# Moving the output stores to ScalarE's queue, letting attention run two batches ahead, and making loads wait for output transposes, in a fused attention and two-layer kernel

## The chip, the cores and the metric

The kernel runs on one core of a Trainium2 chip. The metric is the device time of one execution in microseconds (us); lower is better. A quoted time is a median over executions. A ratio is the mean time of one kernel's fast runs over the mean of the other's fast runs of the same rounds on the same chip, so it is not quite the ratio of the medians quoted beside it. A run is fast unless it lies over 1.5% above the fastest of its kernel.

## The reference

```python
def _attn_ref(q, k, v):              # B, H, S, D = 8, 8, 576, 64
    scores = 1/sqrt(D) * q @ k^T
    # heads 0-3: causal window of 32; heads 4-7: causal window of 128, every 4th key
    attn = softmax(where(mask, scores, -1e9))
    return attn @ v

def _moe_ref(x, w_in, w_out):        # x 4608x512, w_in 512x2048, w_out 2048x512
    h = x @ w_in
    g = h * sigmoid(h)
    return g @ w_out
# x is the attention output with the heads of a token put side by side
```

## The kernel before

All matmuls of attention and of the two layers are issued from one loop. A small model of the engines (`plan`), which runs while the program is built, picks the next step for TensorE; each step's other instructions, the DMAs too, are recorded when the model reaches them. An engine's queue therefore holds its instructions in the order in which the model recorded them.

The words used below:

- **Cast**: GpSimd DMAs that read k and q of a batch as f32 and write them as f16 to a buffer in DRAM (`kq_s`).
- **Turn** of a batch: four DMA transposes on SyncE that bring its k and q from `kq_s` into `nat` and `kqT`.
- **Loads** after a turn: GpSimd waits on a small copy (`fence`) until the turn has landed, then starts v of that batch (`vraw`, `vp`) and the cast of the next.
- **Output transpose**: attention's results (`oP`, `oD`) of batches 2 to 7 are stored to `x_s` in DRAM and read back transposed into `xA` or `xR`, the input of layer 1. A group of layer 1 or 2 has 512 tokens; a batch has 576. Groups 0 and 1 need no output transpose.

```python
    XR = 3                                   # buffers xR
    # ...
    def issue_turn(b):
        # ... (cut)
            nc.sync.dma_start_transpose(out=dst[:, None, :], in_=win)          # nat, x2
        # ... (cut)
            nc.sync.dma_start_transpose(out=kqTs[b % 2][:, i], in_=rows)       # kqT, x2

    def turn_gen(b):
        yield "DMA", max(0.0, TURN_AT.get(b, 0.0) - plan.now)
        issue_turn(b)
        count(("L", b - 2), 2, lambda: loads_after(b))
        yield "DMA", 9.0

    def loads_after(b):
        for i in range(2):
            nc.gpsimd.tensor_copy(fence[:, i : i + 1], kqTs[b % 2][:, i, 1, HN * M - 1 :])
        issue_v(b)
        if b + 1 < B:
            issue_cast(b + 1)

    def group_gen(g):                        # the output transpose of group g
        t0 = max(g * GT, PEB * S)
        n = (g + 1) * GT - t0
        nc.sync.dma_start_transpose(out=x_of(g)[:, :, GT - n :], in_=x_s[t0 : t0 + n])
        yield "DMA", 8.0

    def stored(b):                           # called after each of four stores to x_s
        def then():
            for g in range(NG):
                if need[g] == b:
                    plan.push(groups[g], group_gen(g), plan.now)

        count(("O", b), 4, then)
    # ...
            # after the last score step of batch b: the turn of batch b + 2
            if kind == "S" and b + 2 < B:
                st.after = lambda: count(
                    ("S", b), NS, lambda: plan.push(turned[b + 2], turn_gen(b + 2), plan.t)
                )
    # ... end of a y tile in layer 2
            ob = o32.tile([P, DM], F32, tag="ob", bufs=2, name=f"ob_{g}_{tb}")
            nc.scalar.activation(ob, y, AF.Copy, scale=0.5)
            nc.sync.dma_start(out=out[t0 + tb * P : t0 + (tb + 1) * P], in_=ob)
    # ... which attention steps may be picked while layer 1 is at group g1
        cands = [(att, it, 1.0) for it in att[:LOOK] if it[0] <= g1 + 1]
```

The softmax here doesn't subtract the row's maximum and nothing guards it: scores larger than these inputs give would overflow.

## Time and profile before

| | before |
|---|---|
| time, median (4 runs) | 355.88 us |
| span of the profiled run | 352.8 us |
| mean granted TensorE clock | 0.966 |
| TensorE (PE) busy | 305.7 us, 87% |
| stretches at half clock | 24 us (83.95 to 90.78, 114.67 to 128.33, 152.2 to 155.6) |

The lines that carry the reading stand in the prediction. The question is where TensorE stands still. The prediction's **ledger** and **lag**, which it explains, serve for that: the place of a step in the ledger is the full-clock work ahead of it, in us; a jump of the lag is a stall or half-clock work, and the lag of the last step sets the time.

### The profile page before, as it was taken

The page shows a single profiled execution, that of the slowest core. Times are in us where ns is not written, and L with a number is a line of the kernel's source. Part 1 is how long each engine was busy: PE and PEld are TensorE (multiplying, and loading weights), DVE is VectorE, ACT ScalarE, POOL GpSimd, SP SyncE. Part 2 cuts the span into 40 slices and gives each one's busy share as a digit, 9 for nine tenths or more (in the row PEclk, how much of TensorE's full clock was granted, in tenths as well). Part 3 has the DMA queues.
Part 4 walks back from the last instruction along what each step waited for, and adds up shares of the span by engine and source line. Part 5 has one row for each costly group of instructions (what it writes and reads, how often), then busy time and mean ns, then how long its engine had stood idle before and what let it go on. Part 6 is the DMA issues. An engine that isn't in the chain of part 4 may idle for free.

```text
span 352.8 us, 5672 instructions
## 1 busy us (share of the span) xinstructions
PE 305.7 (87%) x2200; PEld 148.0 (42%) x2200; DVE 201.7 (57%) x477; ACT 153.5 (44%) x258; POOL 48.2 (14%) x76
## 2 busy tenths in 40 slices
PE   0678998992987199789998999999999999999995
PEld 0553544440443044334544444444444444444442
DVE  5594779771775055648866756966675255155100
ACT  1455763442443044445455445545445344244211
POOL 8725000503204002300050030000000000000000
PEclk9999999997899579989999999999999999999999
DMA  8999999999999999995999999051227100100121
GB/s 111 188 205 201 196 190 201 128 192 187 194 199 142 165 233 197 151 163 86 210 156 224 235 172 144 19 123 41 87 64 149 61 0 30 61 30 30 61 82 67
DMA packets 115898, 47.41 MB, mean 134 GB/s; under 512 B 82592, under 2 KB 111264, under 8 KB 115872
## 3 DMA queue, kind: packets, MB, share of 16 engines
q0 software_dynamic: 47152, 19.92, 47.8%
q1 hardware_dynamic: 68720, 27.14, 35.7%
q8 instruction: 17, 0.28, 0.3%
q14 instruction: 9, 0.07, 0.1%
HBM read 39.84 MB, written 20.05 MB: 170 GB/s over the span
## 4 chain that ended last, share of the span: by engine, by line
PE 73%; DMA 14%; DVE 6%; ACT 4%; SPq 1%; issue 1%; POOL 1%; ACTq 0%; POOLq 0%
PE h L611 33%; PE y L639 32%; DMA xR<-x_s 5%; DMA xA<-x_s 3%; DMA x_s<-oD 3%; PE s L413 2%; DMA nat<-in_q_dram 2%; PE av_d L449 2%; DVE oD L453 1%; PE av_p L449 1%; DVE gT L622 1%; SPq L135 1%; ACT th L620 1%; DVE oP L453 1%; ACT ob L650 1%; ACT probs L421 1%
## 5 line engine op out<-in xcount | busy, mean ns | idle before, releaser
L622 DVE SCALAR_TENSOR_TENSOR gT<-th,h 128x512 f16<-128x512 f32 x144 | 97.9, 684 | 92.7 <-ACT th L620 92.7
L639 PE MATMUL y<-w_out,gT 128*128 128x512 f16 x576 | 141.0, 383 | 8.5 <-ACT ob L650 8.1
L620 ACT ACTIVATE th<-h 128x512 f32<-128x512 f32 x144 | 86.2, 599 | 102.0 <-PE h L611 98.7
L611 PE MATMUL h<-xR,w_in 128*128 128x512 f16 x384 | 93.7, 383 | 4.4 <-DMA xR<-x_s 4.3
L611 PEld LDWEIGHTS <-w_in 128*128 128x128 f16 x576 | 54.8, 100 | 81.3 <-issue 22.0
L639 PEld LDWEIGHTS <-gT 128*128 128x128 f16 x576 | 53.6, 98 | 68.5 <-issue 10.2
L611 PE MATMUL h<-xA,w_in 128*128 128x512 f16 x192 | 51.2, 404 | 13.3 <-DMA xA<-x_s 10.2
L421 ACT ACTIVATE probs<-s 128x768 f16<-128x768 f32 (+2 forms) x45 | 36.4, 810 | 22.3 <-PE s L413 22.3
L650 ACT ACTIVATE ob<-y 128x512 f32<-128x512 f32 x36 | 21.5, 597 | 55.1 <-PE y L639 45.3
L449 PEld LDWEIGHTS <-probs 128*128 128x128 f16 x448 | 23.4, 103 | 15.7 <-issue 2.5
L453 DVE TENSOR_TENSOR oD<-av_d,rcps 72x256 f16<-72x256 f32 x64 | 26.9, 421 | 2.2
L300 POOL COPY fence<-kqT 128x1 f16<-128x1 f16 x12 | 2.4, 202 | 142.8 <-DMA kqT<-kq_s 142.8
L453 DVE TENSOR_TENSOR oP<-av_p,rcps 96x256 f16<-96x256 f32 x48 | 20.2, 421 | 1.6
L449 PE MATMUL av_d<-vd,probs 128*128 128x65 f16 x256 | 15.7, 201 | 1.0 <-DVE rcps L452 0.6
L452 DVE RECIPROCAL rcps<-av_p 96x4 f32<-96x4 f32 x48 | 8.4, 174 | 13.2 <-PE av_p L449 13.0
L428 DVE TENSOR_TENSOR probs<-probs,mask_d 128x864 f16<-128x864 f16 (+1 forms) x24 | 13.2, 551 | 3.1 <-ACT probs L421 2.5
L428 DVE TENSOR_TENSOR probs<-probs,mask_p 128x768 f16<-128x768 f16 x24 | 13.3, 554 | 2.6 <-ACT probs L421 2.1
L449 PE MATMUL av_p<-vp,probs 128*128 128x65 f16 x192 | 13.3, 202 | 1.5 <-DVE probs L428 0.9
L452 DVE RECIPROCAL rcps<-av_d 72x4 f32<-72x4 f32 x64 | 11.0, 172 | 5.0 <-PE av_d L449 4.9
L383 PE MATMUL td<-ident,nat 96*128 96x96 f16 x48 | 4.3, 242 | 10.9 <-DMA nat<-in_k_dram 6.8
L155 POOL DMA_DIRECT2D vp<-in_v_dram x8 | 11.5, 1441 | 1.7 <-DMA nat<-in_q_dram 1.6
L141 POOL DMA_DIRECT2D vraw<-in_v_dram x16 | 10.8, 678 | 4.7 <-DVE oD L453 2.5
(60 smaller groups left out, 117.2 us busy)
## 6 DMA issues: line engine op xcount, KB each, us to landing
out_dram<-ob SPq DMA_DIRECT2D x36, 256.0 KB, 2.1
kq_s<-in_k_dram POOLq DMA_DIRECT2D x6, 576.0 KB, 13.0
kq_s<-in_q_dram POOLq DMA_DIRECT2D x6, 576.0 KB, 15.1
vp<-in_v_dram POOLq DMA_DIRECT2D x7, 384.0 KB, 9.9
w_in<-in_moe_w_in_dram POOLq DMA_DIRECT2D x4, 512.0 KB, 11.9
w_out<-in_moe_w_out_dram POOLq DMA_DIRECT2D x4, 512.0 KB, 16.5
vraw<-in_v_dram POOLq DMA_DIRECT2D x8, 224.0 KB, 5.7
x_s<-oP SPq DMA_DIRECT2D x12, 144.0 KB, 2.6
```

The lines of the kernel that those rows point to most:

```text
L141: nc.gpsimd.dma_start(out=vraw[p0 : p0 + m1 - m0, ab].rearrange("p h r d -> p h (r d)"), in_=src[m0:m1],)
L155: nc.gpsimd.dma_start(out=vp[:, j0:, :D], in_=win)
L421: nc.scalar.activation(p2, both[:, :, :n], AF.Exp, scale=scale)
L428: nc.vector.tensor_tensor(p2, p2, mk, ALU.mult)
L449: nc.tensor.matmul(a[:, i, : D + 1], lhs(i), rhs(i), start=True, stop=True)
L452: nc.vector.reciprocal(rcp[:n], a[:n, :, D : D + 1])
L453: nc.vector.tensor_tensor(o, a[:n, :, :D], rcp[:n, :, None].broadcast_to([n, HN, D]), ALU.mult)
L611: nc.tensor.matmul(h, w_in16[:, c, f * P : (f + 1) * P], x_g[:, c], start=(c == 0), stop=(c == HP - 1),)
L620: nc.scalar.activation(th, h, AF.Tanh, scale=0.5)
L622: nc.vector.scalar_tensor_tensor(gTs[g][:, f], th, 1.0, h, ALU.add, ALU.mult)
L639: nc.tensor.matmul(y, gTs[g][:, f, tb * P : (tb + 1) * P], w_out16[:, f], start=(f == 0), stop=(f == NFF - 1),)
L650: nc.scalar.activation(ob, y, AF.Copy, scale=0.5)
```

## The change

Its intent is to take the output stores out of SyncE's queue, where they stand behind transposes; to give the model more attention work to pick from; and to keep the loads of a batch from running beside an output transpose that layer 1 waits for. It also gives `xR` a fourth buffer, and lets the model start turns and loads, and take v as arrived, from what it has recorded so far, where before it used fixed times for some of them.

```diff
-    XR = 3
+    XR = 4
...
-    ARRIVE = {0: (8.5, 15.0), 1: (33.0, 47.0), 2: (60.0, 70.0), 3: (80.0, 90.0)}
-    TURN_AT = {2: 51.0, 3: 72.0}
+    ARRIVE = {0: (8.5, 15.0), 1: (33.0, 47.0)}
...
     def turn_gen(b):
-        yield "DMA", max(0.0, TURN_AT.get(b, 0.0) - plan.now)
         issue_turn(b)
-        count(("L", b - 2), 2, lambda: loads_after(b))
         yield "DMA", 9.0
+        count(("L", b), 3 if b >= 2 * PEB else 2, lambda: start_loads(b))
...
-    def loads_after(b):
+    def loads_gen(b):
         for i in range(2):
             nc.gpsimd.tensor_copy(fence[:, i : i + 1], kqTs[b % 2][:, i, 1, HN * M - 1 :])
+        if b >= 2 * PEB:
+            nc.gpsimd.tensor_copy(fence[:, 2:3], x_of(b - 2)[:, HP - 1, GT - 1 :])
         issue_v(b)
         if b + 1 < B:
             issue_cast(b + 1)
+        yield "DMA", 7.0
+        v_in[b].done = plan.now
+        yield "DMA", 6.0
+        if b + 1 < B:
+            count(("T", b + 1), 2, lambda: start_turn(b + 1))
...
     def group_gen(g):
...
-        yield "DMA", 8.0
+        yield "DMA", 5.0
+        b = need[g]
+        if g == b and b + 2 < B:
+            count(("L", b + 2), 3, lambda: start_loads(b + 2))
...
-            nc.sync.dma_start(out=out[t0 + tb * P : t0 + (tb + 1) * P], in_=ob)
+            nc.scalar.dma_start(out=out[t0 + tb * P : t0 + (tb + 1) * P], in_=ob)
...
-        cands = [(att, it, 1.0) for it in att[:LOOK] if it[0] <= g1 + 1]
+        cands = [(att, it, 1.0) for it in att[:LOOK] if it[0] <= g1 + 2]
```

More of the change, by code (lines that the diff above doesn't have):

```diff
@@ L90 @@
     }
-    fence = cpool.tile([P, 2], F16, name="fence")
+    fence = cpool.tile([P, 4], F16, name="fence")
     mask_p = cpool.tile([P, 6, QB], F16, name="mask_p")
@@ L275, in count, with at_t @@
             then()
+    def at_t(then):
+        plan.now = plan.t
+        then()
     SP_BLOCKS = [[(j, hp) for j in (2 * i, 2 * i + 1) for hp in range(HP // 2)] for i in range(3)]
@@ L285 @@
     need = {g: ((g + 1) * GT - 1) // S for g in range(NG)}
+    v_in = {b: Step(None, 0.0) for b in range(PEB, B)}
     turned = {b: Step(None, 0.0) for b in range(PEB, B)}
@@ L292, in turn_gen, with start_turn @@
     def turn_gen(b):
-        yield "DMA", max(0.0, TURN_AT.get(b, 0.0) - plan.now)
         issue_turn(b)
-        count(("L", b - 2), 2, lambda: loads_after(b))
         yield "DMA", 9.0
-    def loads_after(b):
+        count(("L", b), 3 if b >= 2 * PEB else 2, lambda: start_loads(b))
+    def start_turn(b):
+        plan.push(turned[b], turn_gen(b), plan.now)
+    def loads_gen(b):
         for i in range(2):
             nc.gpsimd.tensor_copy(fence[:, i : i + 1], kqTs[b % 2][:, i, 1, HN * M - 1 :])
+        if b >= 2 * PEB:
+            nc.gpsimd.tensor_copy(fence[:, 2:3], x_of(b - 2)[:, HP - 1, GT - 1 :])
         issue_v(b)
@@ L303, in loads_after, with start_loads, first_cast @@
             issue_cast(b + 1)
+        yield "DMA", 7.0
[3 more added lines that the diff above has]
+            count(("T", b + 1), 2, lambda: start_turn(b + 1))
+    def start_loads(b):
+        plan.push(Step(None, 0.0), loads_gen(b), plan.now)
+    def first_cast():
+        yield "DMA", 52.0
+        count(("T", PEB), 2, lambda: start_turn(PEB))
     def group_gen(g):
@@ L322, in attention @@
         pe_path = b < PEB
-        at_qk, at_v = ARRIVE.get(b, (0.0, 0.0))
+        at_qk, at_v = ARRIVE[b] if pe_path else (0.0, v_in[b])
         vp, vd = vps[b % NV], vds[b % NV]
@@ L588, in attention @@
                 st.after = lambda: count(
-                    ("S", b), NS, lambda: plan.push(turned[b + 2], turn_gen(b + 2), plan.t)
+                    ("S", b), NS, lambda: at_t(lambda: count(("T", b + 2), 2, lambda: start_turn(b + 2)))
                 )
@@ L597, in attention @@
                         ("V", b), NB + 2 * DIL,
-                        lambda: count(("L", b), 2, lambda: loads_after(b + 2)),
+                        lambda: at_t(
+                            lambda: count(
+                                ("L", b + 2), 3 if b >= PEB else 2, lambda: start_loads(b + 2)
+                            )
+                        ),
                     )
@@ L665, in layer2 @@
         return steps
+    plan.push(Step(None, 0.0), first_cast(), 0.0)
     att = []
```

## The prediction

> **What bounds the kernel now.** I read the page first, then the waits of TensorE, then in order of time the SyncE queue, GpSimd and the stretches in which TensorE stands still. TensorE (PE) is the bound: two dense layers of 576 matmuls each, with the attention of eight batches fitted between them.
>
> ```profile
> PE 305.7 (87%) x2200; PEld 148.0 (42%) x2200; DVE 201.7 (57%) x477; ACT 153.5 (44%) x258; POOL 48.2 (14%) x76
> PEclk9999999997899579989999999999999999999999
> ...
> PE h L611 <- DMA xA<-x_s: 10.2, 1, 10.2
> PE y L639 <- ACT ob L650: 8.1, 5, 6.6
> ...
> PE h L611 <- DMA xR<-x_s: 4.3, 2, 3.2
> ```
>
> What can be won lies in a few stalls between 80 and 190 us, each followed by half-clock matmuls (the dips of PEclk). Four matmuls of 512 columns take 0.86 us at full clock. As a ledger I add up TensorE's work in program order: 0.865 us for each step of four (h or y), 0.3 for a score unit, 0.125 for an attention product, a little for the transposes of batches 0 and 1. It gives 284.2 us in all. The start of an instruction minus its place in the ledger I call the lag. In the kernel before it is 28.9 us at batch 2's first scores (65.1 us), jumps by 6.8 at 86.5 us and by 10.3 at 122.6 us, is 62 after 187 us, and ends at 64.5. The last matmul ends at 284.2 + 64.5 = 348.7; the span adds 4.1, and the time (355.1) another 2.3.
>
> The first stall belongs to the queue, the second to a transfer. SyncE, in order of time:
>
> ```profile
> 79.31 3.95 SPq L135 DMA_TRANSPOSE kqT<-kq_s  x2
> 83.37 0.99 SPq L651 DMA_DIRECT2D out_dram<-ob  x2
> ...
> 98.87 5.82 SPq L131 DMA_TRANSPOSE nat<-kq_s  x2
> 104.80 3.48 SPq L135 DMA_TRANSPOSE kqT<-kq_s  x2
> 108.37 1.92 SPq L486 DMA_DIRECT2D x_s<-oD  x2
> ...
> 112.59 2.40 SPq L308 DMA_TRANSPOSE xA<-x_s  x1
> ```
>
> An output store stood behind the input transposes ("turn") of batch 3; ScalarE waited 9.8 us for its buffer, TensorE 6.6 us for ScalarE. Then the output transpose of batch 2 was issued only after the turn of batch 4, at 112.59, and TensorE stood until it had landed:
>
> ```profile
> 122.59 1.87 PE L611 MATMUL h<-xA,w_in 128*128 128x512 f16 x4 [10.19 <-DMA xA<-x_s]
> ```
>
> It took 10 us because the loads of the next batch ran beside it. A later one that ran alone was issued at 233.73, and its traffic was over before 238; the last three columns are the clock, the DMA share and GB/s:
>
> ```profile
> 237.00:238.00 1.00, 1.00 (x7) 0.45 (x5) 0.09 (x1) 0.51 (x1) 0.00 (x0) 1.00 0.72 161
> 238.00:239.00 1.00, 1.00 (x6) 0.43 (x5) 0.70 (x2) 0.69 (x2) 0.00 (x0) 1.00 0.00 0
> ```
>
> The loads themselves, on GpSimd:
>
> ```profile
> 61.30 0.19 POOL L300 COPY fence<-kqT 128x1 f16<-128x1 f16 x1 [0.92 <-DMA kqT<-kq_s]
> 61.83 1.34 POOL L141 DMA_DIRECT2D vraw<-in_v_dram  x2 [0.34 <-DVE oD L453]
> 63.16 1.44 POOL L155 DMA_DIRECT2D vp<-in_v_dram  x1
> 64.58 0.80 POOL L118 DMA_DIRECT2D kq_s<-in_k_dram  x1
> ```
>
> From the fence's end (61.5) it takes 9.4 us until v is in (the landing in the trace is 70.85) and 12.3 us until the first cast has landed and the next turn starts (73.83).
>
> **What the skill says.** "DMA: Bandwidth & Descriptors", section Issuing engines are not separate DMA queues: DMAs started by ScalarE, SyncE or GpSimd run on the same 16 DMA engines; another issuer saves only sequencer time. So stores on ScalarE bring no bandwidth, only a way round SyncE's queue; the trace agrees in that loads from GpSimd stretched a transpose from SyncE from some 5 to 10 us. "PSUM — Partial Sum Buffer", section Engine vs sequencer instructions: ScalarE's queue is strictly first in, first out. So a store that waits holds up the activations behind it; the trace has no store on ScalarE yet, but shows the same on SyncE, where two stores spread over 13.27 us from 144.99. "TensorE: Matmul & The Clock Gate", Part 1: after an idle window of about 3.4 us the clock is half. The trace agrees: half clock from 83.95 to 90.78 and 114.67 to 128.33, two and four windows.
>
> **The change, part by part.** 36 stores leave SyncE, where one issue took 0.34 us, for ScalarE: 36 x 0.34 = 12.2 us more on an engine that is 44% busy, none of it on the path except where a store waits. This removes the 6.8 us stall at 80 us with its half-clock matmuls, and the 13 us that stores held the queue at 145.
>
> Attention may run two batches ahead. The instruction order of the changed kernel shows what comes of it: group 2's first h is now at ledger 63.4 instead of 70.9, batch 4's last product at 91.8 instead of 113.4, batch 7's first scores at 149.2 instead of 176.8. But in SyncE's order batch b-2's last stores and its output transpose still stand behind the turn of batch b, as before. Turn 4 still starts near 98 (its casts follow turn 3, and nothing ahead of that changes), so the first output transpose is issued about 112. Alone it takes 5 us: landed at 117 instead of 122.6. TensorE arrives at 63.4 + 38 = 101 (lag 28.9, plus 5 for batch 2's v, wanted at 65.5 and there at 70.9, plus some 4 of half clock and batch 3's v) and waits 16 us. Lag 117 - 63.4 = 53.6, with 3 of half clock 56.6. Five us earlier in time, but 7.5 of work behind: a small loss.
>
> The third part is the dear one. Loads of batch b now wait for the output transpose of b-2, which stands behind turn b. That makes one serial chain for each batch: turn start to issue of the output transpose 13.5 us (98.87 to 112.59, 127.87 to 141.52, later 13.0 and 11.9), transpose 5, fence 0.5, first cast 12.3: 31.3 us. Before, the starts were 25 to 37 apart, with queueing. From 98 I get turns at 98, 129.3, 160.6 and 191.9 for batches 4 to 7 (before 98.9, 127.9, 164.7, 193.5). v of batch 5 is there at 129.3 + 18.5 + 0.5 + 9.4 = 157.7; its first product is at ledger 95.1, which TensorE reaches at 152: 5.6 us stall, 2 of half clock, lag 65. v of batches 6 and 7 at 189 and 220, at ledger 122.0 and 152.4, ask for lags of 67 and 68.
>
> One wait is worse. The HW DMAs of SyncE and ScalarE take eight completion semaphores in turn, and a store waits for the earlier user of its own. In the built program the second store of group 2 waits for the first transpose of turn 7. It stands behind the y that ends at ledger 115.3, reached at 115.3 + 65 = 180. That transpose starts at 191.9 and lands 5.3 later, at 197.2. ScalarE stands still 16 us; TensorE can run to ledger 117.9 on its two h buffers. Then a tanh (0.60), a product on VectorE (0.69) and hops: 198.8, lag 81. With 3 of half clock, and the slow growth of 2.5 that the kernel before shows from 187 on, 86.5. Sum: 284.2 + 86.5 + 4.1 + 2.3 = 377. Each term leans to late, so I say 374.
>
> **Rivals.** First, as intended: stalls go, lag near 32 at 80 us and 36 at the end, time 327. For it speaks that the stalls of before are 21 us and the clock loss 6 to 7; against it, that the first output transpose is still behind turn 4. Lag 53.6 there, with 3 of half clock and 2 of growth, gives 284.2 + 58.6 + 6.4 = 349 even if nothing waits later. Second, the serial chain counts but the semaphore wait falls away, because turn 7 comes sooner: lag 68 at batch 7, 71 at the end, time 361. Third, the chain is shorter by 2 us a batch (transposes and casts run undisturbed): then turn 7's first transpose lands at 191, and the time is 371 with that wait, 355 without. Fourth, store issues slow ScalarE throughout: 12 us spread over 300, mostly hidden; 2 us at most.
>
> **Range and chances.** The semaphore wait is read from the program and comes up unless turn 7 is 16 us early, so most weight lies at 366 to 380. The low end is the chain alone (360); the high end the chain with 33 us a batch (384). Faster by over 2% needs under 348, below even the first rival's floor: 0.04. Within 2% (348 to 362) needs the semaphore wait gone: 0.16. Slower: 0.80.
>
> **What would show it.** Right: stores on ScalarE, no 6.6 us wait for ob at 80; the first output transpose in 5 us instead of 10, with TensorE waiting 14 to 17 us before it; turns some 31 us apart; a TensorE wait of about 5 us for batch 5's v; a ScalarE idle of some 15 us around 180 to 197 at a store, ended by a nat transpose; mean clock below 0.966. Wrong: turns 25 us apart or the output transpose ahead of the turn, which would make the first rival; no ScalarE idle near 190, the second; turns right but ScalarE busy with issues, the fourth.

## The result, and the profile after

The changed kernel takes 370.17 us (368.85 to 372.12, 4 runs) against 355.88 us (354.62 to 359.16, 4 runs): ratio 1.0391, 95% interval 1.0304 to 1.0479. The profiled run's span is 368.1 us, its clock 0.940. The page's busy line and clock row of the changed kernel:

```profile
PE 307.8 (84%) x2200; PEld 149.1 (41%) x2200; DVE 198.8 (54%) x477; ACT 153.8 (42%) x258; POOL 48.9 (13%) x80
PEclk9999999779975999879957999999999999999999
```

PE is busy 2 us more than before and the rest of the loss is standing still. ScalarE's busy time is unchanged, but busy time does not count the issuing of DMAs. The half clock now covers 44 us (68.8 to 79.1, 106.4 to 120.0, 154.2 to 161.0 and 184.9 to 198.5).

TensorE's waits in the changed kernel (engine, line, what ended the wait, total us, count, longest):

```profile
PE h L638 <- DVE gT L649: 13.0, 4, 12.0
PE av_p L472 <- DMA vp<-in_v_dram: 12.7, 2, 7.0
PE h L638 <- DMA xA<-x_s: 12.5, 1, 12.5
...
PE y L666 <- ACT ob L677: 0.7, 2, 0.4
```

The 6.6 us for the output buffer at 80 us are gone (0.7 is left of 8.1). In their place stand two waits for v, which the kernel before did not have, and one of 12.0 us for VectorE. VectorE is not its cause. The chain of work that ended last, followed through that stretch (start, duration, what), shows it:

```profile
170.69 5.05 DMA xR<-x_s
...
179.16 8.16 DMA kq_s<-in_k_dram
...
187.40 5.09 DMA nat<-kq_s
...
192.56 0.34 ACTq L678
...
193.00 0.60 ACT th L647
...
193.63 0.70 DVE gT L649
...
194.37 1.86 PE h L638 x4
```

An output transpose lands; the fence lets the loads go; the cast lands; turn 7's first transpose starts and lands; only then is a store issued on ScalarE (ACTq L678); and behind that store stand the tanh, VectorE's product and TensorE. In the built program this store, of the second y tile of group 2, uses the completion semaphore of turn 7's first transpose and waits for it. SyncE's and ScalarE's DMAs take eight such semaphores in rotation. The semaphore numbers in the trace agree: the eight are 111 to 118, and both of these DMAs have 116. The store's data had been ready since 180.4.

SyncE's queue in the changed kernel (start, duration, engine, line, operation, out<-in, count):

```profile
99.76 6.13 SPq L131 DMA_TRANSPOSE nat<-kq_s  x2
...
108.87 1.91 SPq L509 DMA_DIRECT2D x_s<-oD  x2
113.07 1.42 SPq L328 DMA_TRANSPOSE xA<-x_s  x1
...
129.13 6.58 SPq L131 DMA_TRANSPOSE nat<-kq_s  x2
```

No output store is left in it. The first output transpose is still issued after turn 4, at 113.07 (before: 112.59), but now runs without loads beside it: TensorE resumes at 116.73, 3.7 us after the issue, where before this took 10.0 us. The turns start at 99.8, 129.1, 160.1 and 187.4.

The jumps of the lag, in us, with the kernels of the experiments that matter for them (a dash is less than 1):

| stall of TensorE | before | changed | e3 | e7 | e10 | e12 |
|---|---|---|---|---|---|---|
| v of batch 2 | – | 7.0 | 6.9 | 6.0 | – | – |
| output buffer (store behind turn 3) | 6.8 | – | – | – | 7.2 | – |
| first output transpose (group 2) | 10.4 | 12.6 | 12.3 | 4.5 | – | – |
| second output transpose (group 3) | 3.3 | – | 2.1 | – | – | 6.6 |
| v of batch 5 | – | 5.7 | – | – | – | – |
| ScalarE behind turn 7's transpose | – | 12.2 | – | – | – | – |
| lag of the last step | 64.5 | 79.9 | 58.0 | 49.4 | 46.4 | 45.8 |
| time of the profiled run | 354.6 | 369.8 | 347.9 | 339.4 | 336.5 | 335.9 |

From before to changed the lag of the last step grows by 15.4 us and the profiled time by 15.2.

### The profile page after: what moved, and what is told of

The parts are those of the page before. It is cut to its first block, busy times and chain, and to the rows that moved or that the text cites.

```text
span 368.1 us, 5678 instructions
## 1 busy us (share of the span) xinstructions
PE 307.8 (84%) x2200; PEld 149.1 (41%) x2200; DVE 198.8 (54%) x477; ACT 153.8 (42%) x258; POOL 48.9 (13%) x80
## 4 chain that ended last, share of the span: by engine, by line
PE 64%; DMA 22%; POOL 4%; DVE 3%; SPq 2%; issue 2%; ACT 2%; ACTq 0%; POOLq 0%
PE y L666 30%; PE h L638 29%; DMA vp<-in_v_dram 4%; DMA w_out<-in_moe_w_out_dram 4%; DMA xR<-x_s 3%; DMA w_in<-in_moe_w_in_dram 3%; DMA kq_s<-in_k_dram 2%; PE s L436 2%; DMA x_s<-oD 2%; SPq L131 1%; PE av_p L472 1%; DMA nat<-kq_s 1%; POOL vraw L141 1%; PE av_d L472 1%; DMA xA<-x_s 1%
## 5 line engine op out<-in xcount | busy, mean ns | idle before, releaser
L666 PEld LDWEIGHTS <-gT 128*128 128x128 f16 x576 | 54.5, 99 | 62.2 <-issue 4.3
L638 PE MATMUL h<-xA,w_in 128*128 128x512 f16 x192 | 52.5, 406 | 14.3 <-DMA xA<-x_s 12.5
L444 ACT ACTIVATE probs<-s 128x768 f16<-128x768 f32 (+2 forms) x45 | 36.4, 810 | 17.6 <-PE s L436 15.5
L472 PEld LDWEIGHTS <-probs 128*128 128x128 f16 x448 | 23.6, 103 | 27.6 <-issue 13.3
(62 smaller groups left out, 116.7 us busy)
```

Source lines behind the costliest of these rows:

```text
L444: nc.scalar.activation(p2, both[:, :, :n], AF.Exp, scale=scale)
L472: nc.tensor.matmul(a[:, i, : D + 1], lhs(i), rhs(i), start=True, stop=True)
L638: nc.tensor.matmul(h, w_in16[:, c, f * P : (f + 1) * P], x_g[:, c], start=(c == 0), stop=(c == HP - 1),)
L666: nc.tensor.matmul(y, gTs[g][:, f, tb * P : (tb + 1) * P], w_out16[:, f], start=(f == 0), stop=(f == NFF - 1),)
```

## The experiments

Twelve kernels ran, on four chips, each beside the kernel before. The theory: the loss comes from attention running two batches ahead together with the chain that waiting loads make, and shows as the waits for batch 5's v and for turn 7. The rivals: the stores on ScalarE cost it; or the loads' waiting costs it by itself.

### The parts of the change

**e1_no_fence**: the changed kernel, with loads that do not wait for the output transpose. TensorE's order is the same.

```diff
-        if b >= 2 * PEB:
-            nc.gpsimd.tensor_copy(fence[:, 2:3], x_of(b - 2)[:, HP - 1, GT - 1 :])
```

> The changed kernel without the one GpSimd copy that makes loads wait for the output transpose; the order on TensorE is the same instruction for instruction. Chain theory: the first output transpose runs beside the loads again and lands near 122.6 instead of 116.7 (TensorE waits 6 us more there), but batch 5's v comes some 6 us earlier and its 5.7 us stall goes; turn 7 starts near 181 instead of 187, so the ScalarE wait at the store shrinks from 12.6 to about 7. Time about 363 (360 to 366). Rival, the waiting of the loads is the whole loss: 356 or less, with no ScalarE wait over 3 us.

Measured: 369.12 us (4 runs) against 354.83 (7 runs), ratio 1.0382 (1.0294 to 1.0469). **A miss**: nothing is won. SyncE's queue of e1:

```profile
113.21 2.49 SPq L326 DMA_TRANSPOSE xA<-x_s  x1
...
132.69 0.84 SPq L507 DMA_DIRECT2D x_s<-oD  x1
133.63 6.94 SPq L131 DMA_TRANSPOSE nat<-kq_s  x2
```

The output transpose now runs beside the loads and lands at 123.5 (10.3 us), so the wait of group 2 grows to 20.0 us. Turn 5 does not start earlier but at 133.6: in SyncE's order it stands behind a store of batch 3's results, which TensorE, standing at group 2, produces late. The waits for batch 5's v (0.7) and behind ScalarE (a jump of 8.5) do shrink; the one loss makes up for the other gains.

**e2_stores_sync**: the changed kernel with its stores back on SyncE.

```diff
-            nc.scalar.dma_start(out=out[t0 + tb * P : t0 + (tb + 1) * P], in_=ob)
+            nc.sync.dma_start(out=out[t0 + tb * P : t0 + (tb + 1) * P], in_=ob)
```

> The changed kernel with the output stores back on SyncE's queue, TensorE's order unchanged. Chain theory: the store of group 2's second tile then stands behind turn 7 and an output transpose in SyncE's queue, issued near 202; the fourth tile's activation waits for that buffer from about 190 to 204, so the stall of 12 us comes back a few us later under another name; time 370 (366 to 374). Rival, store issues or their waits on ScalarE are the loss as such: 358 or less.

Measured: 367.65 us, ratio 1.0346 (1.0276 to 1.0416). As expected, and the stores on ScalarE are not the loss. The 12 us come back under another name, since the store waits behind turn 7 in SyncE's queue and ScalarE waits for the buffer. From the waits of TensorE in e2:

```profile
PE y L666 <- ACT ob L677: 12.7, 3, 12.0
```

**e3_one_ahead**: the changed kernel with attention one batch ahead.

```diff
-        cands = [(att, it, 1.0) for it in att[:LOOK] if it[0] <= g1 + 2]
+        cands = [(att, it, 1.0) for it in att[:LOOK] if it[0] <= g1 + 1]
```

> The changed kernel with attention held at one batch ahead again, stores on ScalarE and the waiting loads kept. Chain theory: first output transpose at 116.7 as in the changed kernel, group 2 starts then with the same work done, but batch 5's first product comes at ledger 118 instead of 95 and needs no wait for v, and the stores that share a semaphore with turn 7 come at ledger 144, well after it (near 202 us); no ScalarE wait over 3 us; time 351 (348 to 355), about 1% better than before. Rival, the serial chain of loads alone makes the loss: 365 or more.

Measured: 347.90 us, ratio of the three fast runs 0.9792 (0.9718 to 0.9866); one slow run (354.4) is left out. As expected. The first two stalls stay (6.9 and 12.3 us), at nearly the same times (71.5 and 114.1); after them nothing over 2.2 follows. From the waits of TensorE in e3:

```profile
PE h L638 <- DMA xA<-x_s: 12.2, 1, 12.2
...
PE av_p L472 <- DMA vp<-in_v_dram: 6.8, 1, 6.8
```

Batch 5's v is now wanted at ledger place 118.5 where the changed kernel wants it at 95.1. The second store of group 2 shares its semaphore with a transpose of turn 6, issued at 158.8; its data are ready only at 168.1, and it does not wait. The first two stalls do not come from the two batches ahead: e3 has group 2's first h at place 63.1 and batch 2's first product at 36.6, much as the changed kernel (63.5 and 36.6), where the kernel before has them at 71.0 and 46.2.

**e4_late_record**: the changed kernel, turn 7 recorded 9 us of the model's time later, so that the store of group 2's second tile shares its semaphore with another DMA. TensorE's order is the same.

```diff
     def turn_gen(b):
+        if b == B - 1:
+            yield "DMA", 9.0
         issue_turn(b)
-        yield "DMA", 9.0
+        if b < B - 1:
+            yield "DMA", 9.0
```

> The changed kernel with only turn 7 recorded later in the program (after the last stores of batch 5's attention), so that it takes other completion semaphores; TensorE's order is unchanged, and turn 7 can't start earlier or later than its casts allow (near 187). Semaphore theory: the store of group 2's second tile no longer waits, the 12.6 us on ScalarE and 12.2 us on TensorE go with 2 us of half clock, nothing takes their place up to batch 7's v; time 356 (353 to 359). Rival, ScalarE would be held by something else or batches 6 and 7 wait for v anyway: 366 or more.

Measured: 359.60 us (4 runs), ratio 1.0118 (1.0037 to 1.0199). Turn 7 still runs late (190.3), v of batch 5 still stalls TensorE by 5.1 us, but the store of group 2's second tile no longer waits and the end's lag is 69.7 where it was 79.9. So that semaphore wait is worth about 10 us. The edit moved the sharing and did not end it: the store of group 2's fourth tile now has the semaphore of turn 7's first transpose and leaves 2.8 us after its data are ready (193.46 to 196.25), and TensorE stands 1.9 us for that. The waits of ScalarE put this down to TensorE and so hide it. The time is 3.6 us above what was expected, just outside the range.

**e5_before_act**: the kernel before with only its stores moved to ScalarE.

> The kernel before with the output stores issued by ScalarE and nothing else. Theory of the absorbed gain: the 6.6 us stall near 80 goes, but group 2 still waits for the output transpose behind turn 4, which lands near 122.6 whatever TensorE did before; the wait there grows from 10 to some 17 us; turn 6 still waits for batch 4's stores near 164; time 354 (352 to 357), the same as before. Rival, the removed stall is worth its 7 to 9 us: 347 or less.

Measured over 20 runs: 356.05 us against 355.08 (39 runs), ratio 1.0038 (1.0011 to 1.0065). The stall of 6.8 us goes and the lag at the end is the same to 0.1 us (64.57 and 64.54). The time is as expected, the way to it is not: the wait of group 2 was to grow to some 17 us, and it fell to 8.1. From the waits of TensorE and of ScalarE in e5:

```profile
PE h L611 <- DMA xA<-x_s: 8.1, 1, 8.1
PE h L611 <- DMA xR<-x_s: 7.4, 1, 7.4
```

```profile
ACT probs L421 <- DMA nat<-kq_s: 5.5, 1, 5.5
ACT th L620 <- DMA nat<-kq_s: 3.4, 1, 3.4
```

Two stores on ScalarE wait for transposes of turns 3 and 4 (the same shared semaphores). TensorE stands 2.2 and 4.2 us for them, so just ahead of group 2's wait its lag is what it was (41.1 us, before 41.3). The 2 us that group 2 then waits less are taken back at group 3, which waits 7.4 us for its `xR`, where before the longest was 3.2. So e5 shows one stall traded for others, and not what the stall by itself is worth.

**e8_one_ahead_no_fence**: e3 without the waiting loads (the edits of e3 and e1 together).

> One batch ahead, stores on ScalarE, and loads that do not wait for the output transpose. It asks what the third part is worth once the second is undone. Theory: the output transposes share the engines with the loads again, the first lands near 120 to 122 instead of 114; time 353 (350 to 356), some 5 us worse than with the waiting loads (347.9). Rival, the waiting loads cost as much as they bring: 346 to 349.

Measured: 362.00 us (4 runs), ratio 1.0196 (1.0100 to 1.0293). **A miss by 9 us.** The output transpose takes 9.3 us beside the loads, where in e3 it took 3.7, and group 2's wait grows from 12.2 to 17.6 us. From the waits of TensorE in e8:

```profile
PE h L636 <- DMA xA<-x_s: 17.6, 1, 17.6
```

With the changed kernel, e1 and e3 this makes a square:

| | loads wait | loads do not wait |
|---|---|---|
| two ahead | 370.17 (1.0391) | e1 369.12 (1.0382) |
| one ahead | e3 347.90 (0.9792) | e8 362.00 (1.0196) |

The waiting of the loads is worth 14 us with attention one ahead and nothing with two. Two ahead costs 22 us with it and 7 without. (By the ratios the differences are 14, 21 and 7 us.) So the parts do not add up, and the theory was half right: two ahead loses in both columns, while the waiting loads lose in neither row and gain with one ahead. What makes e8 itself about 2% slower than the kernel before is left of the change (its rules for recording turns and loads, and the order of steps that follows from them); no run takes these apart. The traces show where it is lost: e8 has group 2's first h at place 63.1 where the kernel before has it at 71.0, but its output transpose lands at 121.0 us, hardly sooner than the 122.6 before. The lag behind that wait is 58.0 where it was 51.6, most of the 8 us by which the ends differ.

### The place of the output transpose in SyncE's queue

In every kernel so far the first output transpose is issued after turn 4.

**e6_out_first**: two ahead; the output transpose of batch b is recorded ahead of turn b+2, which waits for it in the model in place of the loads.

```diff
 # loads_gen: the fence on the output transpose is taken out, and its count
-        count(("L", b), 3 if b >= 2 * PEB else 2, lambda: start_loads(b))
+        count(("L", b), 2, lambda: start_loads(b))
 # group_gen, behind dma_start_transpose
-        yield "DMA", 5.0
         b = need[g]
         if g == b and b + 2 < B:
-            count(("L", b + 2), 3, lambda: start_loads(b + 2))
+            count(("T", b + 2), 3, lambda: start_turn(b + 2))
+        yield "DMA", 5.0
 # (and the two other counts of "T" and "L" for batches from 4 on)
```

> The changed kernel with two batches ahead, but in SyncE's queue each output transpose recorded ahead of the turn two batches later (the turn waits for it instead of the loads). Chain theory: the first output transpose is issued near 99 instead of 113 and lands near 105; group 2 waits under 4 us instead of 12.5; loads follow the turn at once, so turns are at about 101, 130, 155, 179; batches 4 and 5 wait some 5 us each for v, because TensorE is now earlier than the loads; time 350 (346 to 355). Rival, transposes are paced by the transfers themselves and their order in the queue does not matter: 365 or more.

Measured: 358.95 us (20 runs), ratio 1.0129 (1.0097 to 1.0161). **A miss by 9 us**, though 11 better than the changed kernel. The first output transpose is issued at 104.16 and group 2's wait falls to 4.4 us. But the wait for batch 5's v grows to 11.9 us: with two ahead it is wanted early, and its load now runs beside an output transpose (that this is what slows it is read from the trace; no run tests it). GpSimd's and SyncE's queues in e6:

```profile
146.54 1.43 POOL L155 DMA_DIRECT2D vp<-in_v_dram  x1
```

```profile
146.76 4.61 SPq L326 DMA_TRANSPOSE xR<-x_s  x1
```

That load landed at 159.82, 13.3 us after its issue; on the changed kernel's page the median is 7.7.

**e7_one_ahead_out_first**: e6 with attention one ahead (e3's edit).

> Output transposes ahead of the turns as in the last one, and attention held at one batch ahead. Chain theory: the wait of group 2 falls from 12.3 to about 2 us, no batch but the second waits for v, no store waits on ScalarE; lag about 45 at the end; time 336 (333 to 341). Rival, with attention at one batch ahead the transposes wait for the attention instead: 346 or more.

Measured: 339.46 us (4 runs) against 355.08, ratio 0.9557 (0.9495 to 0.9619). As expected. The first output transpose is issued at 102.85. Of the stalls in the table two are left, for v of batch 2 (6.0 us) and at the first output transpose (4.5).

**e9_early_v2**: e7 with v of batch 2 started as soon as batch 0's products are done, ahead of the fence on turn 2. TensorE's order is the same.

```diff
 # loads_gen
-        issue_v(b)
+        if b > PEB:
+            issue_v(b)
 # called when batch b's last attention product is started
+    def after_v(b):
+        if b == 0:
+            issue_v(PEB)
+        count(("L", b + 2), 2, lambda: start_loads(b + 2))
```

> This is e7 (one ahead, the output transpose put into the queue before the turn of two batches later) with one load moved: v of batch 2 is started as soon as batch 0's attention products are done, ahead of the wait for turn 2. TensorE's order is that of e7. Theory (the 6.0 us for which e7's TensorE waited for v at batch 2 is a load that started too late, on the chain): that wait goes, batch 2's stores and the first output transpose come some 5 us earlier, the wait of the first matmul of the second group of layer 1 stays under 2 us, turn 2 is 2 to 3 us later at most; time 332 us (328 to 338), the end's lag near 43 where e7 has 49.4. Rival (the chain of turns decides, and turn 2 loses to the load what the products win): the wait comes back at the first output transpose or at a later batch; time 338 to 341, the same as e7's.

Measured: 338.10 us (4 runs) against 358.04 (7 runs), ratio 0.9510 (0.9422 to 0.9599). **The rival was right**: the wait for v goes, and the lag at the end is 49.6 where e7 has 49.4. With the load that came early, turn 2's first transposes held SyncE nearly twice as long. SyncE's line in e7, the same in e9, and ScalarE's queue in e9:

```profile
50.27 6.59 SPq L131 DMA_TRANSPOSE nat<-kq_s  x2
```

```profile
50.09 12.29 SPq L131 DMA_TRANSPOSE nat<-kq_s  x2
```

```profile
62.44 0.39 ACTq L680 DMA_DIRECT2D out_dram<-ob  x1
62.87 0.65 ACT L448 ACTIVATE probs<-s 128x576 f16<-128x576 f32 x1 [6.16 <-DMA nat<-kq_s]
```

In the built program this first store on ScalarE shares its semaphore with turn 2's first transpose, and an exp stood 6.2 us behind it. TensorE lost 4.2 of that, and group 2's wait for its output transpose was 5.5 us.

**e10_before_out_first**: the kernel before, with the order of SyncE's queue as the only change. Nothing of the change is in it, and TensorE's order is that of the kernel before.

```diff
             for g in range(NG):
                 if need[g] == b:
                     plan.push(groups[g], group_gen(g), plan.now)
+            if b + 2 < B:
+                plan.push(turned[b + 2], turn_gen(b + 2), plan.now)
...
-            if kind == "S" and b + 2 < B:
+            if kind == "S" and b < PEB:
```

> The kernel before with one change in the order of SyncE's queue alone: the turn of batch b+2 stands behind the output transposes of batch b, where it stood ahead of them. Stores stay on SyncE, attention one batch ahead, loads as before; TensorE's order is that of the kernel before. Theory (an output transpose behind a turn starts late and lands slowly, and its wait is the dear one): the first output transpose starts near 103 us where it started at 112.6, the second group of layer 1 does not wait 10 us, the half clock behind it goes; time 338 us (334 to 344). Rival (the turns are the chain: put behind the transposes they come later, and the attention of later batches waits for v, kqT or scores as long as was won): 350 us or more.

Measured: 336.46 us (334.46 to 336.83, 4 runs) against 358.04 (7 runs), ratio 0.9446 (0.9333 to 0.9559). As expected. (The record's own class for e10, as for e9 and e11, is "unclear", and 3 of the 7 runs of the kernel before in this call count as slow. But the slowest run of e10 is 16.7 us under the fastest of those 7, and e7 and e12, with the same order of the queue, are classed as faster.) SyncE's queue of e10, to be held against that of the kernel before in the prediction:

```profile
96.42 6.01 SPq L488 DMA_DIRECT2D x_s<-oD  x2
104.70 2.61 SPq L308 DMA_TRANSPOSE xA<-x_s  x1
...
108.04 4.36 SPq L131 DMA_TRANSPOSE nat<-kq_s  x2
```

Turn 4 stands behind the output transpose and starts 9 us later than before, which no score waits for. Group 2 starts at 112.8 without a wait, and the clock row of e10 has one dip where the kernel before has three:

```profile
PEclk9999999999599999999999999999999999999999
```

### The store stall, once the output transpose is out of the way

e10 still has the output-buffer stall (7.0 us at 87 us). Two ways to remove it:

**e11_out_first_act**: e10 with its stores on ScalarE (the change's first part).

> e10 (the kernel before with the turn of batch b+2 put behind the output transposes of batch b) with the change's first part: the stores go from ScalarE. TensorE's order is that of e10. Theory (a stall ahead of the second group of layer 1 is slack that this group's wait for its output transpose takes back): the 7.0 us for which TensorE waits for ob at 87 us go; in their place come waits of 2 to 5 us behind stores that wait on ScalarE for turn 3's first transpose, and a wait of up to 5 us at the second group; time 336 us (332 to 340), the same as e10's within 1%. Rival (the stall of 7.0 us is on the chain): 329 us.

Measured: 338.43 us over all 6 runs (333.04 to 342.17) against 356.34 (11 runs). Three runs counted as slow; the three fast ones (333.0, 335.0, 337.5) give the ratio 0.9517 (0.9421 to 0.9614). No gain over e10 is shown, and the times spread over 9 us, where those of e12 beside it spread over 2.5. The profiled run had a lag of 43.1 at the end, the least of all, so whether a gain is hidden in the spread stays open.

**e12_out_first_ob4**: e10 with four output buffers where it has two; the order of every engine is that of e10.

```diff
-            ob = o32.tile([P, DM], F32, tag="ob", bufs=2, name=f"ob_{g}_{tb}")
+            ob = o32.tile([P, DM], F32, tag="ob", bufs=4, name=f"ob_{g}_{tb}")
```

> e10 with four output buffers where it has two: the store still stands behind turn 3 in SyncE's queue, but ScalarE and TensorE need not wait for it. Every engine's order is that of e10. Theory: the 7.0 us wait of TensorE for ob at 87 us goes; TensorE reaches the second group of layer 1 near 104 us where it came at 111, and waits there some 5 us for the output transpose, which lands near 109; won are 2 us and some half clock: time 334 us (330 to 337). Rival (all of the stall is on the chain): 329 us.

Measured: 334.05 us (333.43 to 335.90, 6 runs) against 356.34, ratio 0.9436 (0.9379 to 0.9493). The time is as expected, the place of the new wait is not. The stall of 7 us goes, group 2 starts at 104.5 and does not wait, since its output transpose moved forward too (100.80, before it 104.70). The time comes back at group 3. From SyncE's and GpSimd's queues and TensorE's waits in e12:

```profile
123.64 5.76 SPq L308 DMA_TRANSPOSE xR<-x_s  x1
```

```profile
117.41 0.80 POOL L118 DMA_DIRECT2D kq_s<-in_k_dram  x1
```

```profile
PE h L613 <- DMA xR<-x_s: 6.6, 1, 6.6
```

The output transpose of group 3 came forward into the casts and took 10.4 us. The intervals of e10 and e12 overlap, so they are not told apart; both beat the kernel before and the changed kernel.

## Why the prediction was right

It said 374 (360 to 384) and slower; the time was 370.2. By its own steps:

- **Stores on ScalarE cost little and remove the 6.8 us stall.** Right as to the stall, which is gone; each store issue takes ScalarE 0.34 us, as said. What the stall is worth by itself e5 does not tell, since other holds of ScalarE took its place; e12 against e10 (2.4 us less by the medians, 0.1% by the ratios, with intervals that overlap) shows no clear gain from losing 7 us of it.
- **The first output transpose stays behind turn 4 and gains 5 us in time but loses in work.** Right. It was issued at 113.07 (said: about 112) and TensorE resumed at 116.7 (said: 117), with a lag of 53.3 (said: 53.6). Some of this is luck: the issue was 1 us later than said, and the transpose took 3.7 us and not 5. The wait was mis-sized: 12.5 us where 16 were said, because TensorE came at 104 and not at 101. Part of that is batch 2's v, which stalled it by 7.0 and not 5: it landed at 73.0, the loads having started 1.5 us later than before. One step here was wrong: the early place of group 2 was put down to the two batches ahead, but e3, one ahead, has it at 63.1 too, so it comes from the model's other rules.
- **A chain of 31.3 us for each batch.** Right in size for two of three: the distances are 29.4, 31.0 and 27.3. In the last the output transpose was issued 10.6 us after the turn's start, not 13.0, and turn 7 came at 187.4, not 191.9.
- **v of batch 5 stalls TensorE by 5.6 us, landing at 157.7.** It landed at 157.1 and stalled it by 5.7.
- **The second store of group 2 holds ScalarE for 16 us.** The mechanism was right, and e4 shows that it is worth 10 us. It held it for 12.6 us, since turn 7 came 4.5 us sooner: the lag when TensorE goes on is 76.4 where 81 was said. From there it grows by 3.5 where 5.5 were allowed. These are the two terms that made the sum too high: the lag at the end is 79.9 where 86.5 were said. (The last term of the sum is also half a us too large: it sets the median of 355.1 against the span of a run that took 354.6.)
- **"The third part is the dear one."** This step was wrong as an account of cause. The chain is there, but taking the waiting loads away (e1) wins nothing: the turns are then held by attention's own stores in SyncE's queue. With attention one ahead the same waiting loads gain 14 us (e3 against e8). What is dear is running two ahead, most of all in their company (e3 against the changed kernel, 22 us; e8 against e1, 7 us): attention then wants batch 5's v 23 us of work earlier, and the model records turn 7 ahead of group 2's stores. The first output transpose comes no sooner for it.
- **The rivals.** The first (stalls go) failed for the reason given, that the output transpose is still behind turn 4; e10 shows that moving it is the gain that the change was after. The second (no semaphore wait, 361) is close to what e4 measured, 359.6. The third (a chain shorter by 2 us a batch, with the semaphore wait: turn 7's first transpose landing at 191, time 371) is nearest to what happened: it landed at 192.5, and the time was 370.2. The fourth (store issues slow ScalarE) is ruled out as the cause of the loss by e2 and e5; the 2 us that it allowed at most are too few for these runs to exclude.

The tail of the range below 348 us was rightly thin: it needed the output transpose ahead of the turn, and the changed kernel does not do that.

## What to carry to other kernels

Before giving a scheduler more freedom, find the transfer on which the bound engine really waits and see what stands ahead of it in its queue: here one reordering of SyncE (e10) took 5.5% off, where three changes around it lost 3.9%. A stall that is removed can come back at a later wait (e12: 7 us at 87 us gone, 6.6 us at group 3 new) or as another hold (e5 and e9: stores that wait on ScalarE), so removing it alone shows little; read from the lag where it comes back. When DMAs of two engines share completion semaphores, look in the built program for what each store will wait on, for a store can hold its engine for a transfer that has nothing to do with it.

## What the Trainium skill lacked or had wrong

- "DMA: Bandwidth & Descriptors", Issuing engines are not separate DMA queues: it says that another issuer saves only sequencer time. The runs agree on the time (e5, 1.0038). It does not say that the order of one issuer's queue can matter far more than issue time: e10 changed that order alone and gained 5.5%.
- No page that I found says how much a DMA transpose and plain loads slow each other. Here the first output transpose took 3.7 us without loads beside it (changed kernel, e3) and 9.3 to 10.3 us beside loads (e8, e1); turn 2's first transposes held SyncE 6.6 us in e7 and 12.3 us beside one more load in e9; a load of v took 13.3 us beside an output transpose where the median is 7.7.
- "DMA: Bandwidth & Descriptors", Latency and other measured facts, gives 261 GB/s for one kernel's DMA transposes. The first output transpose here moves 384 rows of 1 KB, 393 KB, in the 3.6 us from its issue to its landing, some 108 GB/s. The rate is not what differs: in e3, where it ran alone, its busiest microsecond moved 253 GB/s. At this size the whole time from issue to landing is what counts.
- No page that I found says what it costs when the DMAs of two engines take their completion semaphores from one rotation, so that one must wait for the landing of another. That comes from how this program was built and is no law of the chip, but it cost 12.6 us of ScalarE in the changed kernel and 6.2 us in e9.
- "TensorE: Matmul & The Clock Gate", Part 1: it has the clock fall after an idle window of about 3.4 us. The half-clock stretches do last two, three or four times 3.4 us (6.8, 10.2 and 13.7 us in the changed kernel). But the window need not be idle throughout: by the trace's matmul ends, which are modelled, the changed kernel's clock fell at 106.4, 2.1 us after the last matmul (104.3), and e3's at 103.3, 1.3 us after it (102.0). In the 3.4 us ahead TensorE had been busy for 1.3 and 1.7 us. The prediction, which says that the trace agrees, passed over this: its second stretch, at 114.67, began 2.3 us after the last matmul.
